# Loading the second half of a feed-forward weight as unequal pieces on unequal sets of DMA engines

## The chip, the core and the metric

The kernel runs on one core of one Trainium2 chip. The metric is the device time of one execution in microseconds (us). Three runs of the kernel before gave 134.03, 134.13 and 134.23 us, so the median is 134.13. One further execution was taken with the hardware profiler.

## What is computed

One decode step of a transformer layer whose attention and feed-forward block run in parallel on the same normalised input. Two sequences (B = 2), one new token each, D = 576, 32 query heads over 16 key/value heads of 128, a window of the last 2048 cached positions, and a hidden size F = 4608. All data are bfloat16. The reference, cut to what matters:

```python
xn = _layernorm(x, axis=-1)
# attention: the last W = 2048 positions of the cache
q = (xn @ wq) as (B, Hq, 1, Dh)
scores = einsum("bhqd,bhkd->bhqk", q, k[:, :, Sk - W:]) * (Dh ** -0.5)
o = einsum("bhqk,bhkd->bhqd", softmax(scores), v[:, :, Sk - W:])
attn = o.reshape(B, 1, Hq * Dh) @ wo
# feed-forward: squared ReLU
h = xn @ w1 + b1
h = relu(h) ** 2
mlp = h @ w2 + b2
return x + attn + mlp
```

## The kernel before, in words

Every byte is used once: the kernel reads 53.6 MB of caches and weights from memory and computes little on them, so its loads run all the time and the computation follows behind.

**Units of attention.** The work on the caches is cut into 8 units (four groups of four key/value heads, times two sequences). `load_k(u)` and `load_v(u)` (helper `issue_kv`, L103 to L108) each load one 2 MB tile of 128 partitions with 16,384 bytes in each. The tiles rotate through six buffers (`kvpool`, L85). `step(u)` (L387) transposes the keys of unit u on TensorE, computes the scores and the softmax, and between the transposes multiplies the probabilities of unit u - 2 with their values. `issue_flat` (L116) loads a whole weight (wq, w1, wo) as 128 partitions with one contiguous piece in each; the three share one buffer, so wo is issued when the feed-forward block has read w1.

**Order of the loads.** Nearly all loads are issued from SyncE (SP) in the order of the program: k0, wq, k1, v0, k2, v1, k3, then v2, k4 and so on to v5, then w1, k7, v6, v7, and last wo and w2. Small loads go out from ScalarE (ACT): x at L125, b1 at L417 and L418, b2 at L419. b1 is held as 8 rows of 576 elements (1,152 bytes). It is loaded in five pieces, of 2, 2, 2, 1 and 1 rows. The framework puts in all semaphores and waits.

**The feed-forward block.** `mlp_h(w1_sb)` (L356, called at L434) computes the hidden values and leaves them transposed in `hT_sb`, in two halves of 18 rows (FR = 18) of 128 partitions.

**The end.** w2 is seen as `w2_rows` (L208): two halves, 128 partitions, and in each partition 18 rows of 576 elements, which lie one behind another in memory. The first half is one load, `w2a_sb` (L438). The second half is cut by rows: the first nine (R9 = 9) into `w2b_sb`, a buffer of `kvpool` (L437, L439), the other nine into `w2c_sb` in three loads of 6, 2 and 1 rows (W2P, L76; L440 and L441). Every one of these loads has 128 partitions. After the last attention unit (L442 to L444), TensorE adds all products up in one PSUM tile, `out_ps`: 32 rows of wo, 18 of w2a, then 18 of the second half in order, from `w2b_sb` for r < R9 and from `w2c_sb` after that (L445 to L451). `out_acc` (L216) is four matmuls for a row. The sum is copied on ACT (L454) and stored (L455).

Of the kernel before, what the change touches and what calls it, by code (L numbers as in the profile page):

```python
# [16 lines left out]
def kernel(  # L17
# [14 lines left out]
    nc = tc.nc  # L32
    P = 128
    B, Sq, D = A_x.shape
# [38 lines left out]
    WC = Dh // WR  # L73
    FR = L1 // P
    assert HW == 32 * FR and QH * 2 == NC and NC * WC == 32
    W2P = [(9, 15), (15, 17), (17, 18)]  # L76
    R9 = 9
    BS = 16
    MB = BS * (B - 1) + 1
    RM = 32 * (NG4 - 1) + MB  # L80
# [99 lines left out]
    for t0, half, k0, n, pc in ((0, 0, 0, NK, 0), (0, 1, 0, NK, 1), (1, 0, 1, NK - 1, 1), (1, 1, 0, NK - 1, 0)):  # L180
# [11 lines left out]
                          in_=own[:].unsqueeze(2).to_broadcast([P, NC, WC]))  # L192
# [11 lines left out]
                          in_=ident[0:2 * NG4, 0:2 * NG4].rearrange("p (x g) -> p x g", g=NG4).unsqueeze(3)  # L204
# [3 lines left out]
    w2_rows = B_w2.rearrange("(x p r) n -> x p (r n)", x=2, r=FR)  # L208


    w2c_sb = w2pool.tile([P, (FR - R9) * D], BF16, name="w2c")

# [3 lines left out]
    def out_acc(lhsT, rhs, o, start=False, stop=False):  # L216
        for i in range(4):
            matmul(out_ps[32 * i:32 * i + MB, :], lhsT=lhsT, rhs=rhs[:, o * D + i * OQ:o * D + (i + 1) * OQ],
                   start=start, stop=stop, skip_group_check=True, tile_position=(0, 32 * i))
# [167 lines left out]
    def step(u):  # L387
        fin = None
        w = u - 2
        with_pv = w >= 0  # L390
        for g in range(NG):
            transposes(u, g)
            if with_pv and g == 1:
                pv(w, 0, 2)
            if with_pv and g == 2:
                pv(w, 1, 2)
                fin = pv_end(w)
            if g == TG + 1:
                scores(u, 0)
            if g == TG + 2 and fin:  # L400
                fin()
        scores(u, 1)
        softmax(u)
# [10 lines left out]
    softmax(0)  # L414
    load_v(2)
    b1_rows = B_b1.rearrange("(x n) -> x n", n=HW)
    for i0, i1 in ((0, 2), (2, 4), (4, 6), (6, 7), (7, 8)):  # L417
        nc.scalar.dma_start(out=b1_sb[i0:i1, :], in_=b1_rows[i0:i1, :])  # L418
    nc.scalar.dma_start(out=xb_sb[B:B + 1, :], in_=B_b2.rearrange("(o n) -> o n", o=1))  # L419
    step(1)  # L420
# [15 lines left out]
    w2a_sb = w2pool.tile([P, FR * D], BF16, name="w2a")  # L436
    w2b_sb = kvpool.tile([P, R9 * D], BF16, tag="kv", name="w2b")  # L437
    nc.sync.dma_start(out=w2a_sb[:], in_=w2_rows[0])  # L438
    nc.sync.dma_start(out=w2b_sb[:], in_=w2_rows[1, :, 0:R9 * D])  # L439
    for r0, r1 in W2P:  # L440
        nc.sync.dma_start(out=w2c_sb[:, (r0 - R9) * D:(r1 - R9) * D], in_=w2_rows[1, :, r0 * D:r1 * D])  # L441
    step(NU - 1)  # L442
# [6 lines left out]
    for r in range(FR):  # L449
        w, o = (w2b_sb, r) if r < R9 else (w2c_sb, r - R9)  # L450
        out_acc(hT_sb[:, 1, r, :], w, o, stop=(r == FR - 1))  # L451
# [34 lines left out]
```

## Time and profile before

| what | value |
|---|---|
| median of three runs | 134.13 us |
| the profiled execution | 134.06 us |
| its span, first to last instruction | 132.2 us |
| TensorE busy (matmul) | 85.9 us, 65% |
| VectorE busy | 63.2 us, 48% |
| ScalarE busy | 46.7 us, 35% |
| read from memory | 53.62 MB, 406 GB/s over the span |
| packets of SP's load queue | 3456, 95.1% of 16 DMA engines' time |
| issue of w2a, w2b and w2c's first piece on SP | 95.9, 96.4 and 96.9 us |

How to read it: the page's first part gives each engine's busy share, and none of the compute engines is near full. The second part cuts the span into 40 slices of 3.3 us and shows, in tenths, how busy each engine and the 16 DMA engines together were. The third lists the DMA queues: q1 is SP's queue, q10 is ACT's, and q8 and q14 bring instructions to the engines. The fourth follows the work that ended last back to the start. A time such as 127.95 is in microseconds from the start of the span.

### The profile page before, as it was taken

How to read it: one execution, taken by the hardware profiler on the slowest of the kernel's cores; microseconds unless marked ns; L12 is line 12 of the kernel's file. 1: busy time of each engine (PE TensorE's matmuls, PEld its weight loads, DVE VectorE, ACT ScalarE, POOL GpSimd, SP SyncE). 2: the span in 40 equal slices, each digit the busy share in tenths (PEclk: the TensorE clock that was granted, in tenths of full speed). 3: DMA queues.
4: the chain of work that ended last, by engine and by line, in shares of the span. 5: the costliest groups of instructions: out<-in, count | busy, mean ns of one | idle time of the engine just before them, and what ended most of it. 6: DMA issues, size and time to landing. Idle time of an engine off the chain costs nothing.

```text
span 132.2 us, 2284 instructions
## 1 busy us (share of the span) xinstructions
PE 85.9 (65%) x949; PEld 53.0 (40%) x949; DVE 63.2 (48%) x176; ACT 46.7 (35%) x67; POOL 4.9 (4%) x15
## 2 busy tenths in 40 slices
PE   0079419599589687599687698204819972739561
PEld 0069302287345353445353354002417640229350
DVE  7764400344657677457677457520075667550000
ACT  5715400339576094356094346110106632000000
POOL 5000000010010100100100100100000001000000
PEclk9999955959999999779999869855595999555955
DMA  3999899999999999999999999998999999899960
GB/s 115 436 442 514 380 397 417 436 436 407 444 411 451 421 436 426 431 431 411 456 416 434 426 488 402 407 479 382 441 431 431 480 384 491 382 402 442 397 250 1
DMA packets 3499, 53.76 MB, mean 407 GB/s; under 512 B 407, under 2 KB 546, under 8 KB 802
## 3 DMA queue, kind: packets, MB, share of 16 engines
q1 hardware_dynamic: 3456, 53.61, 95.1%
q8 instruction: 7, 0.11, 0.3%
q10 hardware_dynamic: 34, 0.02, 0.0%
q14 instruction: 2, 0.02, 0.0%
HBM read 53.62 MB, written 0.00 MB: 406 GB/s over the span
## 4 chain that ended last, share of the span: by engine, by line
DMA 77%; PE 17%; SPq 1%; DVE 1%; ACT 1%; issue 1%; ACTq 0%; DVEq 0%
DMA w<-in_B_w_dram 24%; DMA w2c<-in_B_w_dram 23%; DMA k<-in_A_k_cache_dram 16%; DMA wq<-in_A_wq_dram 13%; PE kT_ps L97 7%; PE h_ps L94 3%; PE q_ps L94 3%; PE sc_ps L94 1%; PE o_ps L94 1%; PE out_ps L94 1%; DVE qrow L238 1%; SPq L106 0%; ACT qrow L238 0%; DVE qz L254 0%; SPq L438 0%
## 5 line engine op out<-in xcount | busy, mean ns | idle before, releaser
L97 PE MATMUL kT_ps<-ident_f,k 128*128 128x128 f32 x256 | 42.0, 316 | 5.6 <-DMA k<-in_A_k_cache_dram 4.1
L97 PEld LDWEIGHTS kT_ps<-ident_f,k 128*128 128x128 f32 x256 | 33.3, 162 | 19.1 <-issue 10.2
L270 ACT COPY kT<-kT_ps 128x1024 bf16<-128x1024 bf16 x32 | 31.9, 1012 | 18.9 <-PE kT_ps L97 18.8
L272 DVE COPY kT<-kT_ps 128x1024 bf16<-128x1024 bf16 x32 | 21.8, 681 | 6.4 <-PE kT_ps L97 6.0
L94 PE MATMUL sc_ps<-kT,qz 128*32 128x512 bf16 x128 | 9.7, 383 | 6.7 <-DVE kT L272 4.7
L302 ACT ACTIVATE p<-sc_ps,bias 128x512 bf16<-128x512 f32 x8 | 5.5, 687 | 21.3 <-DVE gown L298 21.3
L94 PE MATMUL o_ps<-v,pT 128*32 128x512 bf16 x128 | 11.9, 457 | 0.0
L94 PEld LDWEIGHTS <-xnT 128*4 128x4 bf16 x108 | 3.6, 120 | 15.8 <-issue 14.2
L94 PE MATMUL h_ps<-w,xnT 128*4 128x288 bf16 x72 | 4.4, 435 | 7.2 <-DMA w<-in_B_w_dram 7.2
L305 DVE STREAM_TRANSPOSE pT<-p 128x512 bf16<-128x512 bf16 x8 | 5.7, 710 | 6.2 <-ACT p L302 6.2
L335 DVE SCALAR_TENSOR_TENSOR o<-o_ps,in_s,o 128x128 f32<-128x128 f32 x24 | 8.3, 345 | 0.4
L291 DVE TENSOR_REDUCE m<-sc_ps 128x1 f32<-128x512 f32 x8 | 5.5, 692 | 4.7 <-PE sc_ps L94 4.7
L94 PE MATMUL q_ps<-wq,xnT 128*4 128x512 bf16 x36 | 4.0, 627 | 4.7 <-DMA wq<-in_A_wq_dram 4.7
L375 DVE TENSOR_TENSOR hrow<-t 100x1152 bf16<-100x1152 f32 x2 | 2.6, 1355 | 8.9 <-ACT t L373 8.9
L295 POOL PARTITION_ALL_REDUCE gmax<-m x8 | 2.9, 365 | 105.1 <-DVE m L293 105.1
L94 PE MATMUL op_ps<-o,of_h 128*32 128x129 f32 x16 | 3.7, 316 | 4.6 <-DVE o L335 4.6
L454 ACT CAST fin_sb<-out_ps 113x144 bf16<-113x144 f32 x1 | 0.3, 278 | 17.8 <-PE out_ps L94 17.8
L94 PEld LDWEIGHTS <-qz 128*32 128x32 bf16 x128 | 2.1, 94 | 10.4 <-DVE kT L272 7.2
L97 PE MATMUL pro_ps<-ident,xn_sb 2*128 2x2 bf16 x5 | 0.9, 181 | 6.8 <-DVE xn_sb L171 6.5
L333 DVE TENSOR_SCALAR o<-o_ps,in_s 128x128 f32<-128x128 f32 x8 | 2.7, 343 | 4.7 <-PE o_ps L94 4.7
L94 PE MATMUL out_ps<-wo,ws 128*17 128x144 bf16 x128 | 4.0, 323 | 1.2 <-DVE ws L351 1.2
L94 PEld LDWEIGHTS <-hT_sb 128*17 128x17 bf16 x144 | 3.3, 107 | 3.6 <-issue 3.5
(71 smaller groups left out, 55.3 us busy)
## 6 DMA issues: line engine op xcount, KB each, us to landing
k<-in_A_k_cache_dram SPq DMA_DIRECT2D x8, 2048.0 KB, 18.6
v<-in_A_v_cache_dram SPq DMA_DIRECT2D x8, 2048.0 KB
w<-in_B_w_dram SPq DMA_DIRECT2D x1, 5184.0 KB, 31.6
wq<-in_A_wq_dram SPq DMA_DIRECT2D x1, 4608.0 KB, 17.8
wo<-in_A_wo_dram SPq DMA_DIRECT2D x1, 4608.0 KB, 21.0
w2a<-in_B_w_dram SPq DMA_DIRECT2D x1, 2592.0 KB
w2b<-in_B_w_dram SPq DMA_DIRECT2D x1, 1296.0 KB
w2c<-in_B_w_dram SPq DMA_DIRECT2D x1, 864.0 KB
```

The costliest lines, as they stand in the source:

```text
L94: tc.keep_in_program_order(nc.tensor.matmul(*a, **k))
L97: tc.keep_in_program_order(nc.tensor.transpose(*a, **k))
L238: cp(out=qrow[:, k * QW:(k + 1) * QW].rearrange("p (i a d) -> p i a d", a=2, d=Dh), in_=q_ps[0:RB, k * QW // 2:(k + 1) * QW // 2].rearrang ...
L270: nc.scalar.copy(out=kT, in_=kT_ps[:])
L272: nc.vector.tensor_copy(out=kT, in_=kT_ps[:])
L291: nc.vector.tensor_reduce(out=m1[:], in_=sc_ps[:], axis=AX.X, op=ALU.max)
L295: nc.gpsimd.partition_all_reduce(gmax[:], m2[:], channels=P, reduce_op=ReduceOp.max)
L302: nc.scalar.activation(out=p_sb[:], in_=sc_ps[:], func=ACT.Exp, bias=bias[:, 0:1], scale=scale, accum_out=o1[:, Dh:Dh + 1])
L305: nc.vector.transpose(out=pT[:].rearrange("p j r -> p (j r)"), in_=p_sb[:])
L333: nc.vector.tensor_scalar(scalar1=in_s[:, 0:1], scalar2=None, op0=ALU.mult, **kw)
L335: nc.vector.scalar_tensor_tensor(scalar=in_s[:, k:k + 1], in1=o1[:, 0:Dh], op0=ALU.mult, op1=ALU.add, **kw)
L375: nc.vector.tensor_tensor(out=h4[:, :, k * HB:(k + 1) * HB], in0=t4, in1=t4, op=ALU.mult)
```

## The change

The cut of w2's second half changes from 9, 6, 2 and 1 rows to 11, 4, 2 and 1 rows. The piece of 11 rows is no longer one load of 128 partitions but five loads of 112, 5, 5, 5 and 1 partitions (the list W2S), all issued from SP in this order, between w2a and the pieces of w2c. The matmuls stay the same in number and order; 11 rows instead of nine are read from `w2b_sb`. Separately, b1 is loaded as one piece of 8 rows instead of five pieces.

```diff
-    W2P = [(9, 15), (15, 17), (17, 18)]
-    R9 = 9
+    W2P = [(11, 15), (15, 17), (17, 18)]
+    R9 = 11
+    W2S = [(0, 112), (112, 117), (117, 122), (122, 127), (127, 128)]
...
-    for i0, i1 in ((0, 2), (2, 4), (4, 6), (6, 7), (7, 8)):
+    for i0, i1 in ((0, 8),):
         nc.scalar.dma_start(out=b1_sb[i0:i1, :], in_=b1_rows[i0:i1, :])
...
-    nc.sync.dma_start(out=w2b_sb[:], in_=w2_rows[1, :, 0:R9 * D])
+    for p0, p1 in W2S:
+        nc.sync.dma_start(out=w2b_sb[p0:p1, :], in_=w2_rows[1, p0:p1, 0:R9 * D])
     for r0, r1 in W2P:
         nc.sync.dma_start(out=w2c_sb[:, (r0 - R9) * D:(r1 - R9) * D], in_=w2_rows[1, :, r0 * D:r1 * D])
```

## The prediction

> **What bounds the kernel now.** I read the page's chain first, then its DMA rows, then the tail in short windows and in order of time, then SP's own waits. The chain, the DMA rows and the queues of the page:
>
> ```profile
> DMA 77%; PE 17%; SPq 1%; DVE 1%; ACT 1%; issue 1%; ACTq 0%; DVEq 0%
> ...
> DMA  3999899999999999999999999998999999899960
> ...
> q1 hardware_dynamic: 3456, 53.61, 95.1%
> q8 instruction: 7, 0.11, 0.3%
> q10 hardware_dynamic: 34, 0.02, 0.0%
> q14 instruction: 2, 0.02, 0.0%
> ```
>
> The loads set the time: from 2 us on the 16 DMA engines are busy without a hole until the last two slices, so what counts is when each engine finishes its share. The tail, in windows (stretch, length, busy time of five engines, TensorE clock, DMA share, GB/s):
>
> ```profile
> 126.00:127.00 1.00, 1.00 (x36) 0.89 (x29) 0.00 (x0) 0.00 (x0) 0.00 (x0) 0.50 1.04 410
> 127.00:127.50 0.50, 0.11 (x4) 0.00 (x0) 0.00 (x0) 0.00 (x0) 0.00 (x0) 0.50 0.51 201
> 127.50:128.00 0.50, 0.05 (x4) 0.05 (x7) 0.00 (x0) 0.00 (x0) 0.00 (x0) 0.50 0.43 168
> 128.00:128.50 0.50, 0.50 (x21) 0.50 (x24) 0.00 (x0) 0.00 (x0) 0.00 (x0) 0.50 0.36 127
> ```
>
> Half of the engines are done by 127.0, and a share of 0.36 is six of sixteen still loading at 128.0 to 128.5. That imbalance is all that can be won. The end, in order of time:
>
> ```profile
> 122.77 1.05 PE L94 MATMUL out_ps<-w2a,hT_sb 128*17 128x144 bf16 x54 [0.24 <-DMA w2a<-in_B_w_dram]
> ...
> 124.95 0.48 PE L94 MATMUL out_ps<-w2a,hT_sb 128*17 128x144 bf16 x18 [1.13 <-issue]
> ...
> 125.87 1.24 PE L94 MATMUL out_ps<-w2b,hT_sb 128*17 128x144 bf16 x36 [0.43 <-DMA w2b<-in_B_w_dram]
> ...
> 127.95 1.35 PE L94 MATMUL out_ps<-w2c,hT_sb 128*17 128x144 bf16 x36 [0.84 <-DMA w2c<-in_B_w_dram]
> ...
> 129.34 0.28 ACT L454 CAST fin_sb<-out_ps 113x144 bf16<-113x144 f32 x1 [17.75 <-PE out_ps L94]
> ```
>
> TensorE waits for each piece of w2; after the last one (1 row, landed at 128.96 by the trace's semaphore records) only four matmuls follow, ending at 129.32.
>
> **Which engine is late, and why.** The trace's packet records hold queue, start, duration and size, not the engine. But a packet begins 3 or 4 ns before its predecessor on the same engine ends, and every 128-partition load is 8 data packets and one of 4 bytes per engine, so the records chain into sixteen sequences. Start of the last 4-byte packet of each, in us:
>
> ```
> six, nothing else on them          126.91 126.91 126.95 126.96 126.97 126.98
> carries five b1 rows and b2 (E0)   127.25
> began k0 0.3 late                  127.26
> one 8 KB instruction fetch         127.63 (this is E1, with three b1 rows)  127.76
> one 16 KB instruction fetch        128.41 128.44 128.46 128.48 128.56 128.62
> ```
>
> One 16 KB fetch costs its engine 1.41 to 1.46 us for good, an 8 KB one 0.55 to 0.81, a small row on ACT's queue 0.048 (0.29 over six). The mean is 127.72, so perfect balance would be worth 0.89 us. The change puts more on engines 0 to 4 and less on 5 to 15, so all hangs on which chains those are. E0 and E1 are known from the b1 packets. The others I infer. In the first load E0 and E1 start fifth and sixth. The seven 16 KB fetches (30.1, 48.5, 68.4, 84.6, 106.5, 122.6, 127.0 us) hit the chains that started 9th, 16th, 14th, 15th, 12th, 4th, 3rd; the two 8 KB ones (35.5, 70.3) the 7th and then E1. If successive fetches step down one engine, 12, 11, 10, 9, 8, 7, 6, and 2, 1, the first eight starters are 4, 5, 6, 7, 0, 1, 2, 3 with E0 and E1 where they were found. I take that: the six late chains are engines 7 to 12, and the 127.76 is E2.
>
> [...] b1's loads of 2 and 1 rows gave 2 and 1 data packets, and x, b1, b2 and the output make just the 34 packets of q10. So 112 partitions run on 16 engines with 7 each, 5 on engines 0 to 4, 1 on engine 0. [...] E0's small packets sit one wq packet (1.37 us) apart.
>
> **Part 1, w2b and w2c.** Packet spacing is 767 ns for 20,736 B and 47 for 1,152 B, so 36.8 ns per 1,000 B plus 4.7. An 11-row partition (12,672 B) costs 0.470, a 4-row one 0.174. Before, w2b takes 3.093 on an engine and the six-row piece 2.077, together 5.170. After: 7 x 0.470 + 0.005 = 3.30, and 8 x 0.174 + 0.005 = 1.40, together 4.70: every engine gains 0.47. Three loads of 5 partitions add 3 x 0.475 = 1.43 to engines 0 to 4 (net +0.95), the single partition 0.475 more to engine 0 (net +1.43).
>
> **Part 2, b1.** One load of 8 rows puts one row on each of engines 0 to 7. E0 keeps two small rows of six: -0.19. E1 keeps one of three: -0.10. Engines 2 to 7: +0.05. The four issues that leave ACT (0.27 us each, at 4.4 to 5.6 us) lie beside a table load; nothing near the end moves.
>
> **Sum.** E0 127.25 + 1.43 - 0.19 = 128.49. E1 127.63 + 0.95 - 0.10 = 128.48. E2 127.76 + 0.95 + 0.05 = 128.76. E3 and E4 at most 126.97 + 1.00 = 127.97. The late six at most 128.62 - 0.47 = 128.15. The last is E2, 128.76 against 128.62: the late engines are relieved and a low engine takes their place, +0.14 us. Against the profiled execution (134.06 us, span 132.20, so 1.86 outside it) that is 134.20; against the median of 134.13 it is 134.27.
>
> **TensorE in the tail.** It now needs five loads before w2b's 44 matmuls. E2's third piece ends at 121.53 + 3.30 + 1.43 = 126.26 and lands 0.31 later at 126.57. At w2b's pace (1.24 us for 36, 34 ns) 68 matmuls run to 126.61 + 2.34 = 128.95; the last row lands at 128.76 + 0.34 = 129.10. TensorE stays hidden, by only 0.15 us.
>
> **SP's waits.**
>
> ```profile
> SPq L106 <- DMA k<-in_A_k_cache_dram: 9.8, 2, 6.3
> SPq L106 <- DMA b_sb<-in_B_b_dram: 6.3, 3, 2.3
> SPq L106 <- DMA wq<-in_A_wq_dram: 2.4, 1, 2.4
> ```
>
> The landing records show eight semaphores used in turn: a load is issued once the eighth before it has landed. With four b1 loads fewer, k1, v0, k2, v1 and k3 go out earlier, but queue behind wq, which runs to 18.4 us: no gain. With four w2b loads more, the two-row piece waits for wo (116.6) and the one-row piece for w2a (122.73). The latter then starts by 122.73 + 0.43 issue + 1.4 (k0's issue to its first packet) = 124.6; the first engine wants it at 126.53 - 0.47 = 126.06. Cover 1.5 us. Behind it on SP is nothing. Were it to wait for w2b, it would start by 128.4 and end the loads near 128.8, as E2 does: at most +0.1. The other four issues (0.42 us each) are done 15 us before wo ends.
>
> **Rivals.** A, the forecast: E2 ends last, 134.27, alone 134.10 to 134.40; chance 0.48. B: the 127.76 chain is none of 2 to 4; E0 ends last, -0.13, 134.00; for it, only E0 and E1 are certain; 0.12. C, slower: fetches do not step down and a 16 KB one falls on engines 2 to 4. That chain gains no 0.47 but pays +1.00. The one at 128.41 would reach 129.41, 0.79 later than now: 134.92, with another up to 135.1. It decides as soon as one late chain is among the three. Against it: the start order of E0 and E1 fits the step; 0.18. D, slower: the 1.13 us gap named issue within w2a's matmuls has no cause I can see. Now it is hidden; in the longer run of 72 matmuls it costs all over 0.15: 134.27 + 0.98 = 135.25. Against it: wo's 128 matmuls ran without one; 0.14. E, the relief in full: the fetches miss E1 and E2 and the small loads spread wider than the rule; 128.15, -0.47, 133.66; for it, no row; 0.08.
>
> **Numbers.** Measurement tells 0.2% (0.27 us) from no change: 133.86 to 134.40. Faster: E, 0.08. Same: B and most of A, 0.55. Slower: C, D and A's tail, 0.37. The range reaches from B with some scatter, 133.95, to C, 134.95; E, D and C's worst are left out, about 0.2.
>
> **What would show it.** Right: w2b's last wait ends near 126.6, the DMA share at 128.2 to 128.6 falls from six engines to about three (E0 to E2), the cast starts near 129.5. B: the cast starts near 129.2. C: one engine (share 0.06) still loading at 129. D: a gap of issue among w2b's or w2c's matmuls. E: no loading past 128.2. Wrong altogether: loads of 5 or 1 partitions that spread over other engines, or a hole in the DMA rows before 126.

## The result: 5.1 us slower

The changed kernel takes 139.28 us (median of four runs, 138.95 to 139.93) against 134.18 before: a ratio of 1.0387, 95% interval 1.0346 to 1.0429. The profiled execution took 138.95 us, span 137.1. The forecast was 134.27, no measurable change.

The page of the changed kernel, the rows that answer to those of before; the row GB/s is what the DMA engines moved in each slice:

```profile
DMA 76%; PE 16%; SPq 2%; ACT 1%; DVE 1%; issue 1%; ACTq 0%; DVEq 0%
...
DMA  4999999999999999999999999999999989999950
GB/s 154 392 489 441 420 398 426 421 449 416 428 435 421 445 411 426 449 421 430 440 421 433 518 411 392 447 387 430 430 440 430 495 366 433 454 288 242 186 171 1
...
q1 hardware_dynamic: 3472, 53.61, 95.0%
q8 instruction: 7, 0.11, 0.3%
q10 hardware_dynamic: 34, 0.02, 0.0%
```

The loads still set the time, and the DMA row still has no hole. But a busy engine is not a moving one: in three slices near the end, where the DMA row still has a 9, the engines move 288, 242 and 186 GB/s instead of some 430. The windows of the tail, changed kernel (last two columns DMA share and GB/s):

```profile
116.00:120.00 4.00, 1.99 (x50) 1.59 (x54) 1.57 (x5) 0.00 (x0) 0.00 (x0) 0.50 1.08 467
120.00:122.00 2.00, 2.00 (x78) 2.00 (x72) 0.00 (x0) 0.00 (x0) 0.00 (x0) 0.50 0.99 304
122.00:124.00 2.00, 0.64 (x24) 0.44 (x13) 0.00 (x0) 0.00 (x0) 0.00 (x0) 0.77 0.95 247
124.00:126.00 2.00, 1.05 (x54) 0.85 (x54) 0.00 (x0) 0.00 (x0) 0.00 (x0) 1.00 1.01 255
126.00:128.00 2.00, 0.77 (x18) 0.47 (x17) 0.00 (x0) 0.00 (x0) 0.00 (x0) 0.59 1.06 208
128.00:130.00 2.00, 0.00 (x0) 0.00 (x0) 0.00 (x0) 0.00 (x0) 0.00 (x0) 0.50 0.85 167
130.00:132.00 2.00, 0.25 (x12) 0.28 (x16) 0.00 (x0) 0.00 (x0) 0.00 (x0) 0.50 0.81 244
```

and three of the same windows before the change:

```profile
120.00:122.00 2.00, 2.00 (x78) 2.00 (x72) 0.00 (x0) 0.00 (x0) 0.00 (x0) 0.50 0.83 353
122.00:124.00 2.00, 1.57 (x74) 1.18 (x63) 0.00 (x0) 0.00 (x0) 0.00 (x0) 0.87 0.98 404
124.00:126.00 2.00, 0.62 (x26) 0.42 (x29) 0.00 (x0) 0.00 (x0) 0.00 (x0) 0.98 0.98 412
```

The rate falls after 120 us and is at 247 GB/s against 404 from 122 us on. The first engines come from w2a to the 112-partition piece of w2b at 120.6 us. The end in order of time, changed kernel:

```profile
124.03 1.05 PE L95 MATMUL out_ps<-w2a,hT_sb 128*17 128x144 bf16 x54 [1.39 <-DMA w2a<-in_B_w_dram]
...
126.50 0.77 PE L95 MATMUL out_ps<-w2a,hT_sb 128*17 128x144 bf16 x18 [1.42 <-issue]
...
131.75 1.50 PE L95 MATMUL out_ps<-w2b,hT_sb 128*17 128x144 bf16 x44 [4.48 <-DMA w2b<-in_B_w_dram]
133.02 1.15 PE L95 MATMUL out_ps<-w2c,hT_sb 128*17 128x144 bf16 x28
134.22 0.28 ACT L456 CAST fin_sb<-out_ps 113x144 bf16<-113x144 f32 x1 [22.52 <-PE out_ps L95]
```

w2a comes 1.26 us later than before, and TensorE starts on w2b at 131.75 where the prediction had 126.61. From there it runs through its 72 matmuls without a wait: its cover of 0.15 us is gone, and w2b's landing (the moment its last completion signal arrives) sets the end. The trace's packet records show the slowing: a packet of 12,672 bytes takes 0.82 us in the mean, where it takes 0.474 in the kernel with one load of 128 partitions below, and packets of w2a and w2c beside them become longer too (w2a's up to 1.37 us instead of 0.77).

### The profile page after: what moved, and what is told of

It is laid out like the page before. It is cut to its first block, busy times and chain, and to the rows that moved or that the text cites. A ratio compares the mean times of both kernels' runs of the same rounds, so it can differ in the third digit from the quotient of the medians.

```text
span 137.1 us, 2286 instructions
## 1 busy us (share of the span) xinstructions
PE 86.5 (63%) x949; PEld 52.7 (38%) x949; DVE 63.0 (46%) x176; ACT 46.5 (34%) x67; POOL 4.9 (4%) x15
## 3 DMA queue, kind: packets, MB, share of 16 engines
q1 hardware_dynamic: 3472, 53.61, 95.0%
## 4 chain that ended last, share of the span: by engine, by line
DMA 76%; PE 16%; SPq 2%; ACT 1%; DVE 1%; issue 1%; ACTq 0%; DVEq 0%
DMA w2b<-in_B_w_dram 25%; DMA w<-in_B_w_dram 24%; DMA k<-in_A_k_cache_dram 15%; DMA wq<-in_A_wq_dram 13%; PE kT_ps L98 4%; PE h_ps L95 3%; PE q_ps L95 3%; PE sc_ps L95 2%; PE out_ps L95 2%; PE qT_ps L98 1%; SPq L107 1%; PE o_ps L95 1%; SPq L441 1%; ACT kT L271 1%; DVE qrow L239 1%
## 5 line engine op out<-in xcount | busy, mean ns | idle before, releaser
L98 PE MATMUL kT_ps<-ident_f,k 128*128 128x128 f32 x256 | 41.2, 311 | 5.1 <-ACT kT L271 2.6
L98 PEld LDWEIGHTS kT_ps<-ident_f,k 128*128 128x128 f32 x256 | 32.5, 159 | 19.0 <-issue 8.7
L95 PE MATMUL sc_ps<-kT,qz 128*32 128x512 bf16 x128 | 10.5, 414 | 6.5 <-DVE kT L273 4.7
```

What stands on the lines that cost most here:

```text
L95: tc.keep_in_program_order(nc.tensor.matmul(*a, **k))
L98: tc.keep_in_program_order(nc.tensor.transpose(*a, **k))
```

## The experiments

**Theories.** 1: where a load doesn't cover 128 partitions, the places that its engines write to at the same moment in SBUF, the on-chip memory, make its packets longer. 2: the new pieces read badly from memory, or loads on few engines are slow in themselves. 3: b1's part, or the order in which SP issues, disturbs the queues. The first batch undoes one part at a time.

**One piece of 128 partitions.**

```diff
-    W2S = [(0, 112), (112, 117), (117, 122), (122, 127), (127, 128)]
+    W2S = [(0, 128)]
```

> The changed kernel with the 11 rows loaded as one piece of 128 partitions. Theory 1 (the unequal partition ranges make several DMA engines write into the same part of SBUF, and the packets of those loads take about 0.8 us instead of 0.47): packets of 12,672 bytes back at 0.47 us, time 134.0 to 134.4 us. Theory 2 (the cut at row 11 or the 12,672-byte pieces read badly from memory): packets stay near 0.8 us, time about 137 us or more. Theory 3 (the b1 load in one piece, or SP's later issues, are to blame): stays near 139 us.

134.56 us, ratio 1.0022 (1.0010 to 1.0035), 0.2 us above the range expected for theory 1. The 12,672-byte packets take 0.474 us. So neither the 11 rows nor pieces of 12,672 bytes are to blame, but the way in which the 128 partitions are cut into loads.

**112 and 16 partitions.**

```diff
+    W2S = [(0, 112), (112, 128)]
```

> The changed kernel with the last 16 partitions as one load [...]. Theory 1 (engines collide wherever a load does not have 128 partitions): the 112-partition packets stay near 0.8 us and the time is 136 to 138 us. Rival (the loads on few engines are the trouble, by their own length or because they take the others' bandwidth): 112-partition packets at 0.47 us, time 134.0 to 134.5 us.

139.98 us, ratio 1.0422 (1.0391 to 1.0453), packets 0.89 us in the mean. With one load of 16 partitions in place of the four small ones it is as slow as the change. So the small loads alone are not the trouble; the time lies 2 us above the 136 to 138 that I expected.

**Two halves of 64 partitions.**

```diff
+    W2S = [(0, 64), (64, 128)]
```

> The changed kernel with the 11 rows as two loads of 64 partitions[...]. Theory 1: [...] packets of 0.93 us, w2b 3.7 us longer, time 137.5 to 138.5 us. Rival (any cause on the reading side, or the few-engine loads): packets of 0.47 us, time 134.0 to 134.5 us.

139.83 us, ratio 1.0433 (1.0376 to 1.0490), packets 0.929 us in the mean: twice 0.47. The time lies 1.3 us over the expectation, which had left out that w2a's and w2c's packets become longer too (4,608 bytes: 0.30 in the mean instead of 0.178).

**The b1 part alone, in the kernel before.**

```diff
-    for i0, i1 in ((0, 2), (2, 4), (4, 6), (6, 7), (7, 8)):
+    for i0, i1 in ((0, 8),):
```

> The kernel before with only the b1 part of the change: one load of 8 rows. My reckoning: engine 0 is relieved by 0.2 us but is not the last one, so the time stays within 0.2% of 134.2 us, while k1, v0, k2 and v1 are issued by 5 us without a wait. Theory 3 (the earlier issues disturb the queues): 1 us or more slower.

134.47 us, ratio 1.0021 (1.0009 to 1.0033): a small loss, not a gain, and no 5 us. Its trace also shows which engines were late. b1's eight rows mark eight chains, which the prediction counts as engines 0 to 7, and the chains end at these times (start of the last 4-byte packet, us after the earliest):

```
eight chains with a b1 row   0  0.02  0.05  0.06  0.08  0.11  0.62 (8 KB fetch)  1.00 (8 KB fetch)
eight chains without one     0.26  0.48  1.72  1.75  1.80  1.81  1.85  1.90 (16 KB fetch: the last six)
```

All six late chains (1.72 to 1.90 us) are among the eight without a b1 row, which the prediction counts as engines 8 to 15, and both 8 KB fetches (0.62 and 1.00 us) are on chains with one.

**Which engine writes which partition.** The records hold neither engine nor address of a packet, so which partitions an engine gets in a load of fewer than 128 is not shown. What the runs can vary is which partitions a load covers. The next kernels do that.

**Eight loads of 16 partitions.**

```diff
+    W2S = [(16 * i, 16 * (i + 1)) for i in range(8)]
```

> The changed kernel with the 11 rows as eight loads of 16 partitions[...]. [...] packets of up to 4 x 0.47 = 1.9 us, w2b up to 11 us longer, time 143 to 147 us. If the engines only lose by the number or the shortness of the loads: packets of 0.47 us and under 136 us. If any range other than 128 partitions costs the same: 139 to 141 us as with the halves.

The four runs scatter from 140.75 to 143.59 us. The ratio, 1.0554 (1.0482 to 1.0625), is that of the two faster ones, about 141.6 us: below the 143 to 147 that I expected. The trace is that of the slowest run, so only the order of size of its packets is used: 1.22 us in the mean, up to 1.79. They are longer than those of the halves (0.929 us), but short of four times 0.474, a factor that was the author's estimate.

**The middle 64 partitions first.**

```diff
+    W2S = [(32, 96), (0, 32), (96, 128)]
```

> The changed kernel with the 11 rows as three loads: partitions 32 to 95, then 0 to 31, then 96 to 127. [...] it is as short as a half of the kernel with halves and reads its rows in the same way. Theory 1 [...]: the first 64 packets take 0.47 to 0.6 us, only those of the two later loads 0.9 us; time 135.5 to 138 us. Rival (the reading side, or any load of 64 partitions): all packets near 0.93 us and about 140 us.

138.11 us, ratio 1.0289 (1.0263 to 1.0315), 0.1 us above the expectation. In order of start, the means of each 16 packets of 12,672 bytes are

```
32 to 95, then the rest   0.474 0.474 0.474 0.596 | 0.922 0.912 0.987 1.001
two halves of 64          0.781 1.032 0.951 0.867 | 0.953 0.991 0.927 0.926
```

The middle load is as short as a half and reads the rows of 64 neighbouring partitions in the same way, yet its packets take 0.474 us, as in a load of 128 partitions, until the next load joins them; the first 16 of the two halves take 0.781. That speaks against the reading side; the pair below settles it for the loads on few engines.

**The few-engine loads by themselves, at the same partitions.**

```diff
+    W2S = [(0, 128)]
+    W2X = [(112, 117), (117, 122), (122, 127), (127, 128)]
...
+    extra = kvpool.tile([P, R9 * D], BF16, tag="kv", name="extra")
+    for p0, p1 in W2X:
+        nc.sync.dma_start(out=extra[p0:p1, :], in_=w2_rows[1, p0:p1, 0:R9 * D])
```

> The changed kernel with the 11 rows as one load of 128 partitions, and the four loads on few engines (5, 5, 5 and 1 partitions) added behind it: they read the same rows of partitions 112 to 127 again into a buffer that nobody reads, so the kernel moves 0.2 MB more. This shows the few-engine loads alone. Reckoning of the prediction (each packet 0.47 us): engine 0 gets 1.9 us more from a start of 126.9 and ends 0.2 us after the engines that are last now, so about 134.9 us. Theory 1 [...]: the few-engine packets take 1 to 1.9 us, the 4,608-byte packets beside them suffer too, and the time is 136.5 to 138.5 us; the 128-partition packets stay at 0.47 us.

137.52 us, ratio 1.0248 (1.0231 to 1.0265), as expected for theory 1. Of the 144 packets of 12,672 bytes, 28 take over 0.6 us, up to 1.43. Only 16 of the 144 belong to the extra loads, so some of the 128-partition load are stretched as well, which the expectation had not foreseen.

**The same loads, into partitions four apart.**

```diff
-    for p0, p1 in W2X:
-        nc.sync.dma_start(out=extra[p0:p1, :], in_=w2_rows[1, p0:p1, 0:R9 * D])
+    for i, (p0, p1) in enumerate(W2X):
+        nc.sync.dma_start(out=extra[i:i + 4 * (p1 - p0 - 1) + 1:4, :], in_=w2_rows[1, p0:p1, 0:R9 * D])
```

> The kernel with extra few-engine loads once more: the same rows read, the same bytes, the same engines 0 to 4, but the five destination partitions of a load lie four apart (0, 4, 8, 12, 16 and so on)[...]. Theory 1 [...]: the extra packets are back at 0.47 us, the other engines' 4,608-byte packets at 0.18, engine 0 ends about 0.2 us after the present last ones, 134.6 to 135.3 us. Rival (loads on few engines, or reading the same rows again, are slow in themselves): packets over 1 us and about 137.5 us as before.

134.77 us, ratio 1.0047 (1.0034 to 1.0061). Same bytes, same rows read, same numbers of engines, same count of loads; only the destination partitions differ, and 2.75 us are gone. Windows of the kernel with the extra loads at partitions 112 to 127:

```profile
122.00:124.00 2.00, 2.00 (x72) 1.84 (x68) 0.00 (x0) 0.00 (x0) 0.00 (x0) 0.50 1.02 433
124.00:126.00 2.00, 0.60 (x26) 0.41 (x15) 0.00 (x0) 0.00 (x0) 0.00 (x0) 0.93 1.08 295
126.00:128.00 2.00, 0.48 (x18) 0.29 (x18) 0.00 (x0) 0.00 (x0) 0.00 (x0) 0.93 0.95 156
128.00:130.00 2.00, 0.50 (x20) 0.50 (x23) 0.00 (x0) 0.00 (x0) 0.00 (x0) 0.50 0.91 191
```

and of the kernel with partitions four apart:

```profile
122.00:124.00 2.00, 1.17 (x66) 0.92 (x55) 0.00 (x0) 0.00 (x0) 0.00 (x0) 0.99 0.95 395
124.00:126.00 2.00, 0.59 (x24) 0.29 (x18) 0.00 (x0) 0.00 (x0) 0.00 (x0) 0.86 0.97 411
126.00:128.00 2.00, 1.18 (x44) 1.17 (x44) 0.00 (x0) 0.00 (x0) 0.00 (x0) 0.50 0.88 349
128.00:130.00 2.00, 1.65 (x40) 0.88 (x31) 0.00 (x0) 0.08 (x1) 0.00 (x0) 0.50 0.27 100
```

From 126 to 128 us the first kernel moves 156 GB/s at a DMA share of 0.95, the second 349 at 0.88. In the second kernel the loads on few engines cost what the prediction reckoned: its packets of 12,672 bytes take 0.474 to 0.482 us but for one of 0.95, and those of 4,608 bytes 0.178.

**Two on b1.** The changed kernel with b1 in five pieces again:

```diff
-    for i0, i1 in ((0, 8),):
+    for i0, i1 in ((0, 2), (2, 4), (4, 6), (6, 7), (7, 8)):
```

> The changed kernel with b1 in its five pieces again. If the parts add up, the b1 part is worth 0.3 us of the 5.1: 138.8 to 139.1 us. If b1's part or the earlier issues it brings decide, 134 to 136 us.

140.21 us, ratio 1.0458 (1.0416 to 1.0499), where the changed kernel has 1.0346 to 1.0429. So b1's single load isn't what costs the 5 us. The time lies above the 138.8 to 139.1 expected if the parts add up, but the two intervals overlap, so that the two kernels differ is not shown. The packets were 0.90 us in the mean instead of 0.82, from one trace each; why, no run shows.

The kernel before with b1 in one load and four idle loads from ACT:

```diff
+    idle = const.tile([4, 64], BF16, name="idle")
+    for i in range(4):
+        nc.scalar.dma_start(out=idle[i:i + 1, :], in_=b1_rows[i:i + 1, 0:64])
```

> The kernel before with b1 in one load, and four idle loads of 128 bytes from ACT into a buffer that nobody reads, so that the turn of the semaphores and SP's waits are as before the change. If the 0.3 us of the b1 part comes from the first loads being issued earlier: 134.1 to 134.25 us. If it comes from b1's rows on eight engines: 134.4 to 134.5 us.

134.69 us, ratio 1.0041 (1.0027 to 1.0055), above both ranges expected. SP issues k1 at 8.36 us and v0 at 10.69 again, as before the change, but the loss is no smaller. So the earlier issues are not shown to be its cause; the idle loads may cost something themselves. Where b1's 0.3 us come from stays open.

## Why the prediction was wrong, step by step

**What failed: "An 11-row partition (12,672 B) costs 0.470", and all that multiplies it.** The price was worked out from loads of 128 partitions. For such a load it holds, as the kernel with one piece shows (0.474 us). It was carried to loads for which it doesn't hold (0.82 us in the mean), and with it a second price, the 0.31 us from the end of w2b's data to its landing.

The records show where the time went. The engines that were not late reached w2b on time: eleven of the sixteen had done with w2a by 121.68 us, and the prediction had 121.53 for E2. w2a's own delay of 1.26 us is that of the late engines and no part of this path. The last packet of 12,672 bytes then ended at 130.53 instead of 126.26, which is 4.27 us, and w2b landed 1.13 us after it, at 131.66, which is 0.82 us more than was reckoned. Together that is 5.09 of the 5.14 us by which w2b's first matmul came later than forecast (131.75 against 126.61).

Within the 4.27 us the chains of packets give the split. The chain that ended last left w2a at 121.68, 0.15 us late. Its seven packets of the 112-partition load ran to 127.37, 0.81 us each, which is 2.4 us more than forecast. Its three packets of the loads on few engines took 1.00, 1.13 and 1.02 us, 1.7 us more than forecast. The same chain was the last of all to end, at 133.42. So the forecast was right that an engine with loads of few partitions takes the place of the late ones, and wrong in the price of its packets (1.00 to 1.13 us for 0.470 in those loads).

**How far the cause is shown.** That the partitions written to decide is shown for the loads on few engines, by the pair of kernels with extra loads (137.52 us into neighbouring partitions, 134.77 into partitions four apart). For the halves it rests on the middle load, which has 64 partitions too and packets of 0.474 us. For the 112-partition load the runs show long packets (also without the four small loads, 0.89 us in the mean), but no kernel wrote the same 112 rows to other partitions; that the partitions are the cause there too is the author's estimate. What it is in the chip that makes these writes slow was not shown.

**Packets of another load were slowed too.** The four extra loads write into partitions 112 to 127 alone. Still the 4,608-byte packets of the w2c load, which has 128 partitions, took 0.315 us in the mean and not 0.178, and 88 of the 128 were over 0.2 us, where only 16 of them go to partitions 112 to 127, one packet to a partition. So the slowing spreads to writes into other partitions; by what path, no run here shows.

**The numbers of engines and partitions.** The trace of before has no load of 112 or 5 partitions, so that they run on 16 and 5 engines was not shown by it. The counts agree: w2b's 128 + 16 packets became 112 + 16, 3 x (5 + 5) and 1 + 1, together 160, and the page counts 16 more on SP's queue (3472 against 3456). In the trace of before, the small rows from b1 and b2 put six packets of 1,152 bytes on one chain (E0) and three on another (E1); that 5 partitions take engines 0 to 4 was the author's estimate, and no count shows it.

**The late engines.** The sixteen chains were read rightly: six engines late by a 16 KB fetch (1.72 to 1.90 us in the trace with b1's eight rows), none of them with a b1 row, both 8 KB fetches on chains with one. The kernel with partitions four apart goes further: the five engines of its third load landed at 126.37, 126.38, 126.42, 126.82 and 127.09 us, so two of these five are late, by 0.4 and 0.7 us, which is nearer to an 8 KB fetch (0.55 to 0.81) than to a 16 KB one (1.4). That fits the forecast's E1 and E2, and speaks against rivals B and C. Only the exact count downwards was off: the fetch at 122.6 fell on a chain without a b1 row in the trace with b1's eight rows, not on engine 7. One figure was added up wrongly: the sixteen ends have a mean of 127.66, not 127.72, so perfect balance would be worth 0.96 us; the forecast doesn't use it.

**TensorE's tail.** The gap named issue stayed inside w2a's matmuls (1.42 us) and did not fall into the 72 at the end, which took 2.45 us for 72, 34 ns each as reckoned. Rival D is out as named. But the cover of 0.15 us, given as thin, was overrun: once w2b lands late, the longer last run is on the path.

**SP's waits.** SP's own waits, changed kernel:

```profile
SPq L443 <- DMA wo<-in_A_wo_dram: 10.7, 1, 10.7
...
SPq L443 <- DMA w2a<-in_B_w_dram: 7.0, 1, 7.0
SPq L443 <- DMA v<-in_A_v_cache_dram: 4.6, 1, 4.6
```

That the last two pieces of w2c wait for wo and w2a was forecast. The first of them waits for a v load, as one piece of w2b does (2.8 us), which the prediction left out. The last piece is issued at 124.01, and no hole in the DMA row follows. **b1** was put at no change to the end; it costs 0.3 us alone, more than the 0.14 us by which the sum moved as a whole.

**The rival that was missing.** The slower cases that the prediction named were a misread engine, a gap and a wait. None said that a transfer can be slower because of where it writes (2.75 us between the two kernels with extra loads). The profile of before could not show it, for every large load in it has 128 partitions: loads of another shape were priced from the only shape that was seen.

**Could the change have worked?** With the extra loads at partitions four apart, the time was about what the prediction's prices give (134.77 us measured, 134.9 in the expectation). But the relief needs low engines to write partitions that the late ones would have written. Whether that can be had at those prices was not shown: no kernel here gains from such relief, and none was faster than before.

## What to carry to other kernels

Price a load by which partitions it writes, not only by bytes and number of engines: here a piece of 128 partitions ran 16 engines at 0.474 us a packet, and 112 of 128, two halves, or five neighbouring partitions on five engines took 0.8 to 1.1 us; five partitions four apart took 0.474 to 0.482, but for one packet of 0.95 in that kernel. A DMA share near 1 with falling GB/s was the mark of it in these profiles (0.95 at 156 GB/s from 126 to 128 us in the kernel with extra loads at partitions 112 to 127). Before moving work from late DMA engines to early ones, measure what a packet takes in a load of the shape and the partitions that the move needs.

## What was not expected of the hardware

- The packets of a load of 112 partitions took about 1.7 times as long as those of a load of 128 (0.8 us for 0.474). Why is open.
- Where packets were long, the landing came late as well: 1.13 us after the end of w2b's last data packet in the changed kernel, 0.37 us after that of the last extra load in the kernel with partitions four apart (126.72 to 127.09).
- Four loads of 203 kB in all, on five engines into neighbouring partitions, cost 3.0 us (137.52 against 134.56), and 0.2 us when the partitions lay four apart (134.77).
- A fetch of 16 KB of instructions held one DMA engine back by 1.4 us to the end of the kernel; six of them left the engines 1.7 us apart.
